# Second GEMM of blocks 2 to 8 by seven quarter-block products (Strassen's way) in a fused retention and feed-forward kernel

## The chip, the cores and the metric

The kernel runs on one core of a Trainium2 chip. The metric is the device time of one launch in microseconds. It is given as the median of several runs; one execution was taken with the hardware profiler.

The engines are named as the profile names them: PE is TensorE's matrix multiply, PEld its weight load, DVE is VectorE, ACT is ScalarE, POOL is GpSimd, and SP is the engine that here only issues transfers. Each engine works through its own instructions in the order in which the program gives them.

## The reference

A retention layer (attention without softmax, with a decay by distance) is followed by a feed-forward layer with a hard-swish between its two matrix products:

```python
# q, k, v: (8, 8, 576, 64) float32
scores = (1 / sqrt(64)) * q @ k.transpose(0, 1, 3, 2)
gamma = 1 - 2 ** (-5 - arange(8))                  # one per head
Dmat = where(rel >= 0, gamma ** rel, 0)            # rel = row - column
x = (scores * Dmat) @ v                            # -> (4608, 512) after a transpose of heads
h = x @ w_in                                       # (4608, 512) @ (512, 2048)
g = h * clip(h + 3, 0, 6) / 6
out = g @ w_out                                    # (4608, 2048) @ (2048, 512), float32
```

## The kernel before

All matrix work is in float16 with float32 accumulation in PSUM. The 4608 tokens are cut into nine blocks of 512, numbered 0 to 8. Blocks 0 to 7 are the first 512 tokens of each batch; block 8 is made of the last 64 tokens of all eight.

**Feed-forward.** `gemm1(kb)` makes the first product of block kb in 16 units. A unit (`g1`) is four matmuls of 512 columns into one PSUM bank `ph` (128 of the 2048 hidden columns, transposed), an ACT operation (Relu with a scale) into `u`, and a DVE operation (`scalar_tensor_tensor`) that writes 128 rows of `gt`, the hidden layer of the block, in float16. The second product (`g2`) takes `gt` as the stationary operand and `wout16` as the moving one. It makes four output tiles of 128 tokens x 512, each in 16 matmuls of 512 columns, cut into four parts: 16 units for a block. ACT copies each tile into `osb`, and SP stores it. In block 8 the last tile is made in two halves of 256 columns (`g2_halves`), so that the last copy and store are short.

**Retention.** It is cut into 36 pieces of 128 tokens: four for each batch, and four "rest" pieces of the last 64 tokens of two batches each. A piece is loaded by POOL's queue (`load`: k, q, v). `ahead(c)` prepares it: SP transposes k by DMA, DVE scales q and v in one operation of 1024 columns (`transpose_q`, line 294), and SP transposes the scaled q by DMA. The work proper is in steps. `step4(ended, begun)` finishes one group of pieces and begins the next, in this order on PE: `inter4(ended)` (what the running state gives, into banks o0 and o1), `scores4(begun)` (into `sc`), `update4(begun)` (the change of the state, into `tu` and a bank u1), `intra4(ended)` (what the masked scores give, added to o0 and o1). `outputs4(ended)` then copies o0 and o1 by ACT to the tokens of the next block in `xt16`. On DVE a step leaves the state's sums (`th`, `ta`, `ts`) and, between them, the mask of the scores (`at`, line 418); on ACT, beside the outputs, small copies `tm` of the state.

**Order.** The order is written out by hand. `put(units, steps)` runs a list of units and, after unit j, what `steps[j]` lists (j = -1: ahead of the first). The tables `steps_at` and `ahead_at` place the steps and the preparations in the second GEMM of each block, and `in_gemm1` places preparations and loads in the first. The retention of block kb + 1 runs inside the second GEMM of block kb. `load_from_here` has a group of loads begin only at a given matmul.

**PSUM.** There are eight banks: two for `sc`, one each for `o` and `tu`, and four that go round under the tag `ph`. These four serve the units of both GEMMs and, in every step, o1 and u1. A bank is written again when its last reader is done. `sc` exists once, so a step's scores wait for the mask of the step before.

Of the kernel before, what the change touches and what calls it, by code (L numbers as in the profile page):

```python
# [10 lines left out]
FP32 = mybir.dt.float32  # L11
# [6 lines left out]
def kernel(  # L18
# [59 lines left out]
    wout16 = big.tile([P, NFC, DM], FP16)  # L78
    xt16 = big.tile([P, NCC, NTOK], FP16)

# [90 lines left out]
    def warm(n, cols):  # L171

        w = psum.tile([P, MBLK], FP32, tag="ph", bufs=4, name=f"warm_{warmed[0]}")
        warmed[0] += 1
        for _ in range(n):
            nc.tensor.matmul(w[:, 0:cols], zeros[:, 0:P], zeros[:, 0:cols],
                             start=True, stop=True)
# [34 lines left out]

    def k_by_pe(c, tag="ph"):
        kn = loaded[c]["kn"]
        pk = psum.tile([P, NPAIR, P], FP16, tag=tag, bufs=4 if tag == "ph" else 1,
                       name=f"trk_{c}")
        for p in range(NPAIR):
            nc.tensor.transpose(pk[:, p, :], kn[:, 2 * p:2 * p + 2, :], ident16)  # L218
        nc.scalar.copy(qk_of(c)[:, 1], pk)  # L219

    def q_by_pe(c):
        q16, qk = loaded[c]["q16"], qk_of(c)
        pq = psum.tile([P, NPAIR, P], FP32, tag="ph", bufs=4, name=f"trq_{c}")
        for p in range(NPAIR):
            for h2 in range(2):
                r = slice(h2 * HALF, h2 * HALF + HALF)
                nc.tensor.matmul(pq[r, p, :], q16[:, 2 * p + h2, :], dq[:, 2 * p + h2, :],
                                 start=(p == 0), stop=(p == NPAIR - 1), skip_group_check=True)
        if c == EARLY - 1:
            for p in (0, 2):  # L230
                nc.scalar.copy(qk[:, 0, p:p + 2], pq[:, p:p + 2])
        else:
            nc.scalar.copy(qk[:, 0], pq)
# [17 lines left out]
    def out_last(c):  # L251
        before, qk = st[c]["before"], st[c]["qk"]
        at, vs = st[c]["at"], st[c]["vs"]
        g0 = column_of(c)
        halves = [psum.tile([P, NPAIR, P], FP32, tag="o", name=f"o_{c}"),
                  psum.tile([P, NPAIR, P], FP32, tag="ph", bufs=4, name=f"o2_{c}")]
        for i, o in enumerate(halves):
            for p in range(2):
                nc.tensor.matmul(o[:, p, :], tbd[before][:, 2 * i + p, :], qk[:, 0, 2 * i + p, :],
                                 start=(p == 0), stop=False, skip_group_check=True)  # L260
        for i, o in enumerate(halves):
            for p in range(2):
                for h2 in range(2):
                    r = slice(h2 * HALF, h2 * HALF + HALF)
                    nc.tensor.matmul(o[r, p, :], vs[:, 4 * i + 2 * p + h2, :],
                                     at[:, h2, 2 * i + p, :],
                                     start=False, stop=(p == 1), skip_group_check=True)
            nc.scalar.copy(xt16[:, 2 * i:2 * i + 2, g0:g0 + P], o[:, 0:2, :])

# [43 lines left out]
    def inter(c, tag="o"):  # L313
        kind, b, i, _ = pieces[c]
        o = psum.tile([P, NPAIR, P], FP32, tag=tag, bufs=4 if tag == "ph" else 1, name=f"o_{c}")
        st[c]["o"] = o
# [12 lines left out]
    def intra(c, copy_later=False, more=False):  # L329
        o, at, vs = st[c]["o"], st[c]["at"], st[c]["vs"]  # L330
        for p in range(NPAIR):
            for h2 in range(2):
# [3 lines left out]
                                 stop=(p == NPAIR - 1 and not more), skip_group_check=True)  # L336
        g0 = column_of(c)

        def copy():
            nc.scalar.copy(xt16[:, :, g0:g0 + P], o)  # L340

# [86 lines left out]
    def inter4(cs):  # L428

        o = [psum.tile([P, 2, NPAIR, HALF], FP32, tag="o", name=f"o0_{cs[0]}"),  # L430
             psum.tile([P, 2, NPAIR, HALF], FP32, tag="ph", bufs=4, name=f"o1_{cs[0]}")]
        written = set()
# [39 lines left out]
    def outputs4(cs):  # L472
        o, g0 = st[cs[0]]["o"], column_of(cs[0])
        if len(cs) == 2 and column_of(cs[1]) == g0 + P:
            for half in range(2):
                nc.scalar.copy(  # L476
                    xt16[:, :, g0:g0 + 2 * P].rearrange("e p (j x s) -> e p j x s", j=2, x=2)
                    [:, :, :, half, :], o[half].rearrange("e j p s -> e p j s"))
        else:
            for j, c in enumerate(cs):  # L480
                for half in range(2):
                    g0 = column_of(c) + half * HALF
                    nc.scalar.copy(xt16[:, :, g0:g0 + HALF], o[half][:, j])

    def update4(cs):

        cs = [c for c in cs if pieces[c][0] != "rest"]
        if not cs:
            return
        u = [psum.tile([P, 2, NPAIR, D], FP32, tag="tu", name=f"u0_{cs[0]}"),  # L490
             psum.tile([P, 2, NPAIR, D], FP32, tag="ph", bufs=4, name=f"u1_{cs[0]}")]
        for j, c in enumerate(cs):
# [46 lines left out]
    def g1_mm(kb, ph, fc, dmcs):  # L539
        t0 = kb * MBLK  # L540
        for dmc in dmcs:
            newest[0] = nc.tensor.matmul(  # L542
                ph, win16[:, dmc, P * fc:P * fc + P], xt16[:, dmc, t0:t0 + MBLK],
                start=(dmc == 0), stop=(dmc == NCC - 1))
# [9 lines left out]
    def g1_bank(kb, fc):  # L554
        return psum.tile([P, MBLK], FP32, tag="ph", bufs=4, name=f"ph_{kb}_{fc}")

    def g1(kb, fc, tag=None):
        ph = psum.tile([P, MBLK], FP32, tag=tag, name=f"ph_{kb}_{fc}") if tag else g1_bank(kb, fc)
        g1_mm(kb, ph, fc, range(NCC))
        g1_act(kb, ph, fc)  # L560

    def g1_columns(kb, fc, ph, cols):

        t0 = kb * MBLK
        for dmc in range(NCC):
            nc.tensor.matmul(ph[:, cols], win16[:, dmc, P * fc:P * fc + P],  # L566
                             xt16[:, dmc, t0 + cols.start:t0 + cols.stop],
                             start=(cols.start == 0 and dmc == 0),
# [26 lines left out]
    def g2(kb, mc, part):  # L595
        gt = gts[kb]
        if part == 0:
            pouts[kb, mc] = psum.tile([P, DM], FP32, tag="ph", bufs=4, name=f"pout_{kb}_{mc}")
        pout = pouts[kb, mc]
# [7 lines left out]

    def g2_halves(kb, mc):
        gt = gts[kb]
        W = DM // 2  # L610
        for half in range(2):
            pout = psum.tile([P, W], FP32, tag="ph", bufs=4, name=f"pout_{kb}_{mc}_{half}")
            for fc in range(NFC):
                nc.tensor.matmul(pout, gt[:, fc, P * mc:P * mc + P],  # L614
                                 wout16[:, fc, half * W:half * W + W],
                                 start=(fc == 0), stop=(fc == NFC - 1))
            osb = work.tile([P, W], FP32, tag="osh", bufs=2, name=f"osb_{kb}_{mc}_{half}")
            nc.scalar.copy(osb, pout)
            store(kb, mc, slice(half * W, half * W + W), osb)

# [63 lines left out]
    def first_step(c):  # L684
# [3 lines left out]
        if old:  # L688
            before = state_of.get(b)
            tag, bufs = ("ph", 4) if c == 6 else ("o", 1)  # L690
            o = psum.tile([P, NPAIR, P], FP32, tag=tag, bufs=bufs, name=f"o_{c - 1}")
            st[c - 1].update(o=o, first=True)
# [16 lines left out]
        if new:  # L709
            k_by_pe(c + 1, "ph" if old else "tu")  # L710
        if old:
# [16 lines left out]
    def scores_second(c):  # L728

        qk = st[c]["qk"]  # L730
        banks = [psum.tile([P, NPAIR, P], FP32, tag="ph", bufs=4, name=f"sc{i}_{c}")
                 for i in range(2)]
# [15 lines left out]
    def step(ended, begun):  # L748

        for c, tag in zip(ended, ("o", "ph")):  # L750
            inter(c, tag)
# [91 lines left out]
    i = 0  # L843
    for kb, at in ((2, (4, 8, 12)), (3, (4, 11)), (4, (3, 7, 12)), (5, (4, 11)), (6, (2, 8))):
        for j in at:
            steps_at.setdefault(kb, {})[j] = [(step4, groups[i], groups[i + 1])]
            i += 1
    steps_at[6][12] = [(inter4, groups[i]), (inter_done, groups[i])]
    steps_at[6][13] = [(end4, groups[i])]

    ahead_at = {1: {10: (12,), 11: (13,), 13: (14,), 14: (15,)}, 2: {1: (17,), 3: (18,)},
                3: {0: (21,), 1: (22,), 7: (23,), 8: (24,)}, 4: {0: (27,), 1: (28,)},
                5: {0: (31,), 1: (32,)}, 6: {0: (35,)}}
# [3 lines left out]
                5: {0: [(load_from_here, 29, 32)], 9: [(ahead, 29)], 12: [(ahead, 30)]},  # L857
                6: {0: [(load_from_here, 33, 35)], 9: [(ahead, 33)], 12: [(ahead, 34)]}}
    for kb in range(1, NMB - 1):
        steps = steps_at.get(kb, {})  # L860
        for j, cs in ahead_at.get(kb, {}).items():
            steps.setdefault(j, []).extend((ahead, c) for c in cs)
        put([unit2(kb, mc, part) for mc in range(MBLK // P) for part in range(4)], steps)
        gts.pop(kb)
        gemm1(kb + 1, in_gemm1.get(kb + 1, {}))
    for mc in range(MBLK // P - 1):
        for part in range(4):
            g2(NMB - 1, mc, part)
    g2_halves(NMB - 1, MBLK // P - 1)

# [29 lines left out]
```

## Time and profile before

| | us |
|---|---|
| median of 3 runs (306.27 to 307.74) | 306.35 |
| span of the profiled execution, first to last instruction | 303.8 |
| median less that span | 2.55 |

The profiled execution has no time of its own beside its span; what lies around the span is taken as the difference to the median.

| engine | busy us | share of the span | instructions |
|---|---|---|---|
| PE | 294.0 | 97% | 3035 |
| PEld | 146.4 | 48% | 3035 |
| DVE | 178.5 | 59% | 308 |
| ACT | 167.8 | 55% | 303 |
| POOL | 107.7 | 35% | 134 |

The mean granted clock of TensorE is 0.998. From block 2 on, each first GEMM takes 13.81 to 14.4 us; a second GEMM without retention steps (block 7) takes 13.81 us, and one with them 16.69 to 18.35 us.

A line of groups in the profile reads: source line, engine, operation, output<-inputs, shape, count | busy time, mean ns of one | idle time of the engine before them and what ended it. A line of a timeline reads: start, length, engine, line, operation. Durations of PE overlap (a matmul of 512 columns shows 379 ns, though one starts every 216), so its prices are taken from spacing.

### The profile page before, as it was taken

The page shows a single profiled execution, that of the slowest core. Times are in us where ns is not written, and L with a number is a line of the kernel's source. Part 1 is how long each engine was busy: PE and PEld are TensorE (multiplying, and loading weights), DVE is VectorE, ACT ScalarE, POOL GpSimd, SP SyncE. Part 2 cuts the span into 40 slices and gives each one's busy share as a digit, 9 for nine tenths or more (in the row PEclk, how much of TensorE's full clock was granted, in tenths as well). Part 3 has the DMA queues.
Part 4 walks back from the last instruction along what each step waited for, and adds up shares of the span by engine and source line. Part 5 has one row for each costly group of instructions (what it writes and reads, how often), then busy time and mean ns, then how long its engine had stood idle before and what let it go on. Part 6 is the DMA issues. An engine that isn't in the chain of part 4 may idle for free.

```text
span 303.8 us, 7342 instructions
## 1 busy us (share of the span) xinstructions
PE 294.0 (97%) x3035; PEld 146.4 (48%) x3035; DVE 178.5 (59%) x308; ACT 167.8 (55%) x303; POOL 107.7 (35%) x134
## 2 busy tenths in 40 slices
PE   6989999999999999999999999999999999999994
PEld 2644445544544555445544554445445444444443
DVE  4667526796838775966388767942895057108600
ACT  5557537874467455753585548633773367227511
POOL 8963557359840302930191009600840000000000
PEclk9999999999999999999999999999999999999999
DMA  9999999999999972999599619992992100010022
GB/s 69 144 193 206 190 156 209 163 120 151 187 173 146 155 126 83 116 120 174 142 128 178 115 37 127 140 151 74 107 150 74 71 37 0 35 73 32 1 69 71
DMA packets 153169, 35.61 MB, mean 117 GB/s; under 512 B 143792, under 2 KB 148656, under 8 KB 153136
## 3 DMA queue, kind: packets, MB, share of 16 engines
q0 software_dynamic: 117264, 18.36, 88.7%
q1 hardware_dynamic: 35472, 16.26, 29.6%
q8 instruction: 24, 0.39, 0.5%
q10 hardware_dynamic: 400, 0.52, 0.5%
q14 instruction: 9, 0.07, 0.1%
HBM read 36.70 MB, written 9.44 MB: 152 GB/s over the span
## 4 chain that ended last, share of the span: by engine, by line
PE 87%; DMA 5%; POOL 4%; issue 1%; DVE 1%; ACT 0%; DVEq 0%; POOLq 0%
PE pout L601 39%; PE ph L542 38%; DMA win<-in_moe_w_in_dram 3%; POOL qv L91 2%; DMA qk<-vs 2%; PE o L445 2%; PE o L466 1%; POOL kn L91 1%; PE ph L566 1%; PE sc L412 1%; PE pout L614 1%; PE u L498 1%; PE o L334 1%; PE sc L305 1%; POOL win L95 0%
## 5 line engine op out<-in xcount | busy, mean ns | idle before, releaser
L551 DVE SCALAR_TENSOR_TENSOR gt<-u,ph 128x512 f16<-128x512 f32 x144 | 97.3, 687 | 51.8 <-ACT u L550 50.5
L601 PE MATMUL pout<-wout,gt 128*128 128x512 f16 x560 | 125.9, 379 | 0.0
L542 PE MATMUL ph<-xt,win 128*128 128x512 f16 x560 | 122.7, 379 | 1.0 <-DMA win<-in_moe_w_in_dram 1.0
L550 ACT ACTIVATE u<-ph,cb 128x512 f32<-128x512 f32 x144 | 98.3, 687 | 27.1 <-PE ph L542 26.4
L542 PEld LDWEIGHTS <-win 128*128 128x128 f16 x560 | 54.6, 98 | 67.1 <-DMA win<-in_moe_w_in_dram 1.9
L601 PEld LDWEIGHTS <-gt 128*128 128x128 f16 x560 | 53.1, 98 | 61.5
L91 POOL DMA_DIRECT2D kn<-in_k_dram x40 | 35.3, 887 | 102.8 <-PE ph L542 75.7
L605 ACT COPY osb<-pout 128x512 f32<-128x512 f32 x35 | 20.5, 585 | 60.7 <-PE pout L601 60.7
L91 POOL DMA_DIRECT2D qv<-in_q_dram x40 | 35.2, 885 | 5.3 <-DMA wout<-in_moe_w_out_dram 3.3
L91 POOL DMA_DIRECT2D qv<-in_v_dram x40 | 35.5, 894 | 3.6 <-DMA win<-in_moe_w_in_dram 1.7
L294 DVE TENSOR_TENSOR vs<-qv,gqv 128x1024 f16<-128x1024 f16 x28 | 18.7, 686 | 4.7 <-issue 3.5
L309 DVE TENSOR_TENSOR at<-sc,mask_wide 128x1024 f16<-128x1024 f32 x9 | 11.0, 1222 | 14.1 <-PE sc L305 14.0
L529 DVE TENSOR_TENSOR ta<-u,th 128x256 f32<-128x256 f32 x20 | 8.4, 420 | 12.5 <-ACT th L517 11.7
L418 DVE TENSOR_TENSOR at<-sc,mask 128x1024 f16<-128x1024 f32 x11 | 13.4, 1216 | 2.4 <-PE sc L412 2.4
L514 DVE TENSOR_TENSOR th<-u,ts 128x256 f32<-128x256 f32 x15 | 6.4, 425 | 11.6 <-PE u L498 11.2
L476 ACT CAST xt<-o 128x512 f16<-128x512 f32 x16 | 8.6, 589 | 6.4 <-PE o L466 6.4
L519 ACT CAST tm<-th 128x256 f16<-128x256 f32 x20 | 8.2, 412 | 2.8 <-DVE th L514 2.4
L530 DVE TENSOR_TENSOR ts<-ta,gc 128x256 f16<-128x256 f32 x20 | 8.5, 425 | 0.7
L340 ACT CAST xt<-o 128x512 f16<-128x512 f32 x11 | 6.3, 588 | 3.5 <-PE o L707 1.7
L219 ACT COPY qk<-trk 128x512 f16<-128x512 f16 x8 | 4.7, 586 | 4.7 <-PE trk L218 4.6
L412 PE MATMUL sc<-qk 64*64 64x64 f16 x384 | 6.5, 195 | 0.7 <-DMA qk<-vs 0.7
L457 ACT COPY seen<-o 128x1 f32<-128x1 f32 x13 | 2.1, 159 | 9.0 <-PE o L445 8.9
(90 smaller groups left out, 159.2 us busy)
## 6 DMA issues: line engine op xcount, KB each, us to landing
out_dram<-osb SPq DMA_DIRECT2D x32, 256.0 KB, 2.2
kn<-in_k_dram POOLq DMA_DIRECT2D x32, 128.0 KB, 5.9
qv<-in_q_dram POOLq DMA_DIRECT2D x32, 128.0 KB, 5.9
qv<-in_v_dram POOLq DMA_DIRECT2D x32, 128.0 KB, 6.6
wout<-in_moe_w_out_dram POOLq DMA_DIRECT2D x4, 512.0 KB, 15.2
win<-in_moe_w_in_dram POOLq DMA_DIRECT2D x3, 512.0 KB, 11.7
win<-in_moe_w_in_dram POOLq DMA_DIRECT2D x2, 256.0 KB, 7.4
kn<-in_k_dram POOLq DMA_DIRECT2D x8, 64.0 KB, 4.1
```

The costliest lines, as they stand in the source:

```text
L91: loaded[c]["dma"].append(nc.gpsimd.dma_start(dst[p0:p0 + n], src[b, :, s0:s0 + n, :].rearrange("h s d -> s h d")))
L294: scaled = nc.vector.tensor_tensor(out=vs, in0=loaded[c]["qv"], in1=gqv, op=ALU.mult)
L309: later.append(lambda: nc.vector.tensor_tensor(out=at.rearrange("t a b s -> t (a b) s"), in0=sc.rearrange("t a b s -> t (a b) s"), in1=mas ...
L412: nc.tensor.matmul(sc[rows(half), h2, j, p, :], qk[rows(h2), 1, p, rows(half)], qk[rows(h2), 0, p, rows(half)], start=True, stop=True)
L418: nc.vector.tensor_tensor(out=at.rearrange("t a j p s -> t (a j p) s"), in0=sc.rearrange("t a j p s -> t (a j p) s"), in1=mask64[:, None, ...
L476: nc.scalar.copy(xt16[:, :, g0:g0 + 2 * P].rearrange("e p (j x s) -> e p j x s", j=2, x=2) [:, :, :, half, :], o[half].rearrange("e j p s ...
L530: nc.vector.tensor_tensor(out=ts, in0=ta, in1=scale, op=ALU.mult)
L542: newest[0] = nc.tensor.matmul(ph, win16[:, dmc, P * fc:P * fc + P], xt16[:, dmc, t0:t0 + MBLK], start=(dmc == 0), stop=(dmc == NCC - 1))
L550: nc.scalar.activation(u, ph, ACTF.Relu, bias=cb[:, 0:1], scale=1.0 / 6.0)
L551: nc.vector.scalar_tensor_tensor(out=gts[kb][:, fc, :], in0=u, scalar=1.0, in1=ph, op0=ALU.min, op1=ALU.mult)
L601: nc.tensor.matmul(pout, gt[:, fc, P * mc:P * mc + P], wout16[:, fc, :], start=(fc == 0), stop=(fc == NFC - 1))
L605: nc.scalar.copy(osb, pout)
```

## The change

Blocks 2 to 8 make their second product as follows. The block's hidden layer (512 tokens x 2048) is cut into quarters a(i, j) of 256 tokens x 1024, the weights into quarters w(i, j) of 1024 x 256. In place of eight products of quarters, seven are made, of sums of quarters: s1 to s4 from the hidden layer, made on DVE for each block (`token_sums`), and t1 to t4 from the weights, made once on DVE during block 1's second GEMM (`weight_sums`). Each product is two units of eight matmuls of 256 columns, so a second GEMM has 14 units and 112 matmuls.

Four PSUM banks serve the products, by name: x (three products, one added to the other), z (two), y and v (one each). `bank` hands out the four `ph` banks in turn and passes over those that are held; x and z are held to the end of the block. ACT copies x out after each of its three products (`keep`: m1, u2, u3, float32), and DVE adds such a copy to y, z, v and again z (`total`), which gives the four quarters of the output. Each is stored in one transfer with rows of 1 KB (`store_quarter`). In block 8, z is in the two banks of `sc`, and the last quarter is added and stored in two halves.

`token_sums` s1 and s2 are made in two halves each, behind units 12, 13 and 15 of the block's first GEMM; s3 and s4 are made during the second. The retention steps and some preparations stand behind other units than before. The one large `xt16` gives way to tiles by block (`xt_of`), two in turn and one for block 8; this makes room in SBUF.

```diff
+    def bank(shape, dtype, name):
+        i = next(x for x in ring if x not in held)
+        ring.remove(i)
+        ring.append(i)
+        return psum.tile(shape, dtype, tag=f"ph{i}", name=name)
+    def hold_bank():
+        held.append(ring[-1])
+    def free_banks():
+        for i in held[1:]:
+            ring.remove(i)
+            ring.append(i)
+        held.clear()
...
+        a, b, op = {"t1": (w(0, 1), w(0, 0), ALU.subtract),
+                    "t2": (w(1, 1), t("t1"), ALU.subtract),
+                    "t3": (w(1, 1), w(0, 1), ALU.subtract),
+                    "t4": (w(1, 0), t("t2"), ALU.subtract)}[which]
+        nc.vector.tensor_tensor(out=t(which), in0=a, in1=b, op=op)
...
+    def token_sums(kb, which, c0=0, c1=KH):
...
+                sums[kb, name] = work.tile([P, KH, TH], FP16, tag="sum_" + {"s4": "s1"}.get(name, name), bufs=1,
+                                           name=f"sum_{name}_{kb}")
...
+        x, y, op = {"s1": (lambda: a(1, 0), lambda: a(1, 1), ALU.add),
+                    "s2": (lambda: s("s1")[:, c0:c1], lambda: a(0, 0), ALU.subtract),
+                    "s3": (lambda: a(0, 0), lambda: a(1, 0), ALU.subtract),
+                    "s4": (lambda: a(0, 1), lambda: s("s2")[:, c0:c1], ALU.subtract)}[which]
+        nc.vector.tensor_tensor(out=s(which)[:, c0:c1], in0=x(), in1=y(), op=op)
...
+        def product(name, u, left, right, first):
+            dst = get(name)
+            for c in range(KH):
+                nc.tensor.matmul(dst[:, u, :], left()[:, c, P * u:P * u + P], right[:, c, :],
+                                 start=(first and c == 0 and (u == 0 or last and name == "z")),
+                                 stop=(c == KH - 1), skip_group_check=True)
...
+        def keep(name, src):
+            kept[name] = work.tile([P, 2, NH], FP32, tag="keep_" + {"u3": "m1"}.get(name, name), bufs=1,
+                                   name=f"keep_{name}_{kb}")
+            nc.scalar.copy(kept[name], get(src))
+        def total(i, j, name, src):
+            osb = work.tile([P, 2, NH], FP32, tag="osb", bufs=4, name=f"osb_{kb}_{i}_{j}")
+            nc.vector.tensor_tensor(out=osb, in0=get(src), in1=kept[name], op=ALU.add)
+            store_quarter(kb, i, j, osb)
...
+        plan = [
+            ("x", lambda: a(0, 0), w(0, 0), True, [lambda: keep("m1", "x")]),
+            ("y", lambda: a(0, 1), w(1, 0), True,
+             [lambda: total(0, 0, "m1", "y"), lambda: token_sums(kb, "s3")]),
+            ("x", lambda: s("s2"), wts["t2"], False,
+             [lambda: keep("u2", "x")]),
+            ("z", lambda: s("s1"), wts["t1"], True, [lambda: token_sums(kb, "s4")]),
+            ("x", lambda: s("s3"), wts["t3"], False,
+             [lambda: keep("u3", "x"), lambda: total(1, 1, "u3", "z")]),
+            ("v", lambda: a(1, 1), wts["t4"], True, [lambda: total(1, 0, "u3", "v")]),
+            ("z", lambda: s("s4"), w(1, 1), False, [] if last else
+             [lambda: total(0, 1, "u2", "z"), free_banks]),
+        ]
...
-    for kb, at in ((2, (4, 8, 12)), (3, (4, 11)), (4, (3, 7, 12)), (5, (4, 11)), (6, (2, 8))):
+    for kb, at in ((2, (1, 5, 9)), (3, (3, 9)), (4, (1, 5, 9)), (5, (3, 9)), (6, (1, 7))):
...
-    steps_at[6][12] = [(inter4, groups[i]), (inter_done, groups[i])]
-    steps_at[6][13] = [(end4, groups[i])]
+    steps_at[6][10] = [(inter4, groups[i]), (inter_done, groups[i])]
+    steps_at[6][11] = [(end4, groups[i])]
-    ahead_at = {1: {10: (12,), 11: (13,), 13: (14,), 14: (15,)}, 2: {1: (17,), 3: (18,)},
-                3: {0: (21,), 1: (22,), 7: (23,), 8: (24,)}, 4: {0: (27,), 1: (28,)},
+    ahead_at = {1: {10: (12,), 11: (13,), 13: (14,), 14: (15,)}, 2: {0: (17,), 2: (18,)},
+                3: {0: (21,), 1: (22,), 5: (23,), 6: (24,)}, 4: {1: (27,), 2: (28,)},
                 5: {0: (31,), 1: (32,)}, 6: {0: (35,)}}
...
+    for j, which in ((2, "t1"), (4, "t2"), (9, "t3"), (10, "t4")):
+        steps_at[1].setdefault(j, []).append((weight_sums, which))
+    SEVEN = (2, 3, 4, 5, 6, 7, 8)
...
+            if kb + 1 in SEVEN:
+                for j, which in ((12, "s1"), (13, "s2")):
+                    within.setdefault(j, []).append((token_sums, kb + 1, which, 0, KH // 2))
+                for which in ("s1", "s2"):
+                    within.setdefault(15, []).append((token_sums, kb + 1, which, KH // 2, KH))
```

## The prediction

> **What bounds the kernel now.** I read the page's busy shares, then the windows view over the alternating stretches of the two GEMMs (cut where the matmuls' line changes), then the groups by form, the chain and timelines. Times are in us unless marked ns; T is the start of a block's second GEMM.
>
> ```profile
> PE 294.0 (97%) x3035; PEld 146.4 (48%) x3035; DVE 178.5 (59%) x308; ACT 167.8 (55%) x303; POOL 107.7 (35%) x134
> ```
> ```profile
> 118.56:132.37 13.81, 13.81 (x66) 6.27 (x64) 12.20 (x19) 11.06 (x17) 11.97 (x15) 1.00 1.45 120
> 132.37:149.06 16.69, 16.69 (x297) 8.68 (x296) 9.45 (x16) 6.32 (x15) 0.00 (x0) 1.00 1.53 141
> 149.06:162.87 13.81, 13.81 (x65) 6.27 (x64) 10.35 (x16) 10.86 (x16) 10.49 (x12) 1.00 1.95 145
> 162.87:181.22 18.35, 18.35 (x434) 10.08 (x432) 12.09 (x23) 8.60 (x23) 0.00 (x0) 1.00 0.77 109
> ...
> 195.03:212.61 17.58, 16.93 (x305) 8.81 (x304) 6.89 (x13) 6.45 (x17) 0.00 (x0) 1.00 0.88 118
> ...
> 257.88:271.69 13.81, 13.81 (x65) 6.27 (x64) 1.37 (x2) 2.46 (x5) 0.00 (x0) 1.00 0.15 58
> ```
>
> Columns: stretch, length, busy PE, PEld, DVE, ACT, POOL, granted clock, DMA. Rows: both GEMMs of block 3, both of 4, the second of 5 and of 7. PE idles only in block 5 (0.65): TensorE is the bound, and time taken off it is gained unless a wait takes its place. DVE is the engine to watch: block 3 uses 12.20 + 9.45 = 21.65 of 30.50.
>
> ```profile
> L601 PE MATMUL pout<-wout,gt 128*128 128x512 f16 x560 | 125.9, 379 | 0.0
> ...
> L551 DVE SCALAR_TENSOR_TENSOR gt<-u,ph 128x512 f16<-128x512 f32 x144 | 97.3, 687 | 51.8 <-ACT u L550 50.5
> L294 DVE TENSOR_TENSOR vs<-qv,gqv 128x1024 f16<-128x1024 f16 x28 | 18.7, 686 | 4.7 <-issue 3.5 <-DMA qv<-in_v_dram 1.2
> ...
> L137 DVE TENSOR_TENSOR dq<-ident,gq 128x1024 f16<-128x1024 f16 x1 | 1.2, 1226 | 0.3 <-ACT gq L125 0.3
> ```
> ```profile
> 296.03 3.51 PE pout L614 x32
> ```
>
> Prices: 64 matmuls of 512 columns fill 13.81, 215.8 ns each. In the chain the 32 of 256 columns take 3.51, 109.7 ns each. On DVE a 1024-element f16 operation costs 686 ns.
>
> ```profile
> 138.13 4.71 PE L601 MATMUL pout<-wout,gt 128*128 128x512 f16 x21
> ...
> 138.43 1.07 ACT L476 CAST xt<-o 128x512 f16<-128x512 f32 x2 [0.88 <-PE o L466]
> ...
> 141.32 0.42 DVE L530 TENSOR_TENSOR ts<-ta,gc 128x256 f16<-128x256 f32 x1
> 141.66 1.28 DVE L294 TENSOR_TENSOR vs<-qv,gqv 128x1024 f16<-128x1024 f16 x2
> ...
> 200.91 0.32 PE L412 MATMUL sc<-qk 64*64 64x64 f16 x16 [0.65 <-DMA qk<-vs]
> ```
>
> These timeline rows (start, length) give the rest: a step's outputs are out of PSUM 0.30 + 1.07 after PE has gone on to the next product; a queued DVE operation starts 0.08 before the last one ends (141.66 against 141.74), so 686 ns counts 603 in a full queue; and block 5's step already waits for a transposed q.
>
> **The change, part by part.**
>
> *Products.* A block loses 64 x 215.8 ns = 13.81 and gets 112 x 109.7 = 12.29: -1.52. Block 8 had 48 x 215.8 and 32 x 109.7 = 13.87: -1.58. Seven blocks: **-10.7**, all on PE. This rests on L614's pitch, which hides a weight load of 98 ns with 12 to spare. [...]
>
> *VectorE.* New per block: s1 and s2 in halves (4 x 0.603), s3 and s4 of 2048 elements (512 f16 elements take 418 ns in L205's row, 1024 take 686, so 2048 take 1.22, 1.14 in a queue), four totals from PSUM (L551's size, 4 x 0.603): 7.1. ACT keeps three copies for four: -0.6, hidden. Block 3: 21.65 + 7.1 = 28.8 of 30.50 - 1.52 = 29.0; block 4: 22.4 + 7.1 = 29.5 of 30.6; block 7: 18.9 of 26. So DVE is full in blocks 2 to 4, and its queue, in order, decides who waits. The weight sums (4 x 1.14) fall in block 1's second GEMM, where DVE is busy 10.4 of 16.6: nothing; without that cover, 4.6.
>
> *Banks.* x and z hold two of the four banks. In blocks 2 to 5 the step behind unit 9 takes both others, and v, next on PE, gets the one of the step's o1: it waits for ACT's copies out of it. Price 0.30 + 1.07 = 1.4 (block 3); four narrow copies (L483: 384 ns, 300 for each further one) make it 1.6 in 4 and 5; two make 1.0 in 2: **+5.6**. Before, the bank after a step's was drained long ago.
>
> *Block 2.* DVE's order behind the first GEMM: the last hard-swish product (ACT starts at T + 0.20, takes 0.69, DVE follows 0.17 later, and 0.42 late through the first halves of s1 and s2), the second halves (to T + 3.3), then the mask of the step that opens the block (ends T + 4.5). The next step moves from behind unit 4 (T + 4.8) to behind unit 1 (T + 2.2), and its scores need the one sc tile: PE is there at T + 2.6, **+1.9**, with products y and on queued behind. DVE now runs late: that step's th, ta, ts, th, mask, ta, ts (3.7 by their rows), piece 18's scaling, and only then total 00 at T + 10.2; z gets y's bank and waits **0.75**.
>
> *Block 4.* Likewise: second halves to T + 3.9 (two scalings late in the first GEMM), step 3.7, scalings of 27 and 28 1.2, total 00 done at T + 9.6; PE wants z at T + 8.15: **+1.45**.
>
> *Transposes.* Steps come sooner after the first GEMM, transposes don't. Block 5: q of piece 30 lands at T + 5.85 (200.9), the step behind unit 3 asks at T + 4.3: 1.6, less the 0.65 of before. Block 3: q of 20 landed at T + 4.4, asked for at 3.9: 0.5. **+1.45**. On SP's queue total 00's store, which now waits on DVE, stands ahead of the transposes of 23 and 24; these have the next first GEMM for cover, without it some 2. POOL's loads keep their places.
>
> *Small ones.* Block 3's x waits for its ACT copy behind a step's state copies, 0.15; block 5's y for the last hard-swish product, 0.4; block 6's third pass on x for s3, 0.5; in blocks 7 and 8, z's last pass for ACT's copy and DVE's total (0.9 + 0.8 + hand-over) against v's 1.75, 0.1 each: **+1.25**. The tail is a copy and stores of the same size: nothing. Stores have rows of 1 KB for 2: DMA moves 58 GB/s in block 7, so nothing, at most 0.5 at the end.
>
> *Sum.* -10.7 + 5.6 + (1.9 + 0.75) + 1.45 + 1.45 + 1.25 = **+1.7** on the profile's span of 303.8: 305.5. The runs' median (306.35) is 2.55 above that span, start and end that the change doesn't touch: **308.0**. The waits, which the trace of before can't show, are bounded by nothing (-10.7) and about double (+14.1); I take the walk between, as its rows are of the same operations.
>
> **Rivals.**
> 1. *VectorE keeps up* (faster): only v's waits remain, as nothing stands between step and v: -10.7 + 5.6, **301.2**. For it: in blocks 6 to 8 DVE has a quarter of the time free. Against: 28.8 of 29.0 in block 3. Chance 0.30.
> 2. *Transposes become the bound* (slower): the scalings queue behind sums, so q of pieces 22 and 28 is issued up to 4 later and lands 2.6 (201.49 to 204.06) to 6 after issue. Blocks 3 and 4 need them behind unit 9, near T + 11.6 and T + 13.5, about when they land; from there each us late is a us. 1.5 each: **311.0**. Against: loads have ended by then, so 2.6 is the likelier. Chance 0.13.
> 3. *Sums at one element a cycle* (slower): L137, with one f32 operand, takes 1226 ns for 1024. At that rate sums cost 4.3 more a block; blocks 2 to 4 get DVE's own length (99.6 against 94.9 before), 5 to 8 wait some 2 each for s2 and save 1.5, and 5's v waits 1.6: **314.7**. It decides once a half sum exceeds 0.9. Against: the sums are f16 throughout, as L294. Chance 0.07.
> 4. *The clock drops* (slower): early warm-up matmuls start 427 ns apart (2.018, 2.445), half the later rate. If a stall in each of blocks 2 to 5 brought that back for 3.5, two products' time, each would lose 1.75: **315.0**. The longest gap in the trace is 0.77 and leaves clock 1.00; my longest wait is 1.9. [...] Chance 0.03.
> 5. *No PE time is saved* (slower): weight loads surface and cost 14 ns a matmul, 112 x 14 = 1.57 a block, so the waits alone remain: **318.7**. Against: L614. Chance 0.02.
>
> **How the numbers follow.** The walk has 0.45; with its 12.4 of waits off by 30% either way it spans 304 to 312. This kernel's measurement tells some 0.5% (1.5) from no change. Slower by more: half of the walk (0.23), rivals 3 to 5 (0.12) and most of 2 (0.10): 0.45. Faster: rival 1 and the low end of the walk, 0.34. Within: 0.21. The range 300 to 313 leaves out rivals 3 to 5 (0.12) and the far end of 1 (0.06).
>
> **What would show it.** Products: the second GEMMs of blocks 7 and 8 near 12.4. Banks: four PE waits of 1.0 to 1.6 on ACT's xt copies, just ahead of v. DVE: sums at 686 ns and 1.22; PE waiting for the mask in block 2, for total 00 in 2 and 4. I am wrong if blocks 3 to 5 shrink by 1.5 each (rival 1), or if a single wait exceeds 2.5.

## The result and the profile after

The changed kernel takes **309.90 us** (median of 4 runs, 308.47 to 310.76), the kernel before 306.31 on the same chip (4 runs). The ratio is 1.0122, with a 95% interval of 1.0087 to 1.0156: slower by 1.2%. The profiled execution has a span of 308.9 and is the longest of the four (the others: 306.6, 308.0, 308.2), so its 5.14 over the span of before is more than the 3.6 between the medians.

From the page of after: the engines, and the granted clock by fortieths of the span.

```profile
PE 285.4 (92%) x3355; PEld 179.3 (58%) x3355; DVE 233.6 (76%) x383; ACT 164.1 (53%) x297; POOL 107.7 (35%) x134
...
PEclk9599999999999999999999999997999999999999
```

PE was busy for 97% of its span, now for 92%: the work fell by 8.6, the span rose by 5.1. In the clock's row one slice near 210 has fallen to 7. The windows view (stretch, length, busy PE, PEld, DVE, ACT, POOL, granted clock, DMA) over the second GEMMs of blocks 2, 3, 4, 5, 7 and 8:

```profile
102.43:121.84 19.41, 16.59 (x434) 14.50 (x425) 17.77 (x32) 8.16 (x23) 2.63 (x3) 1.00 0.59 86
...
135.65:152.73 17.08, 15.30 (x346) 13.43 (x345) 15.35 (x25) 6.31 (x15) 0.00 (x0) 1.00 1.45 131
...
166.54:186.74 20.20, 16.92 (x482) 14.99 (x480) 19.34 (x34) 8.73 (x25) 0.00 (x0) 1.00 0.59 87
...
200.55:221.34 20.79, 17.25 (x354) 14.46 (x353) 14.40 (x24) 6.54 (x17) 0.00 (x0) 0.92 0.81 86
...
265.45:277.68 12.23, 12.23 (x113) 10.96 (x112) 7.84 (x11) 2.47 (x5) 0.00 (x0) 1.00 0.13 45
291.49:308.91 17.42, 12.56 (x113) 10.86 (x111) 8.68 (x13) 2.47 (x5) 0.00 (x0) 0.97 0.23 61
```

Block 7, where no retention step stands, takes 12.23 instead of 13.81: the seven products are 1.58 shorter, and 12.23 / 112 is 109.2 ns a matmul. Blocks 2 to 5 have 1.8 to 3.5 in which PE stands still. Block 5 has, besides, a clock of 0.92. The waits of PE (line, what it waited for: us in all, times, longest) name these idle times:

```profile
PE v L717 <- ACT xt L512: 3.4, 3, 1.4
PE sc L442 <- DMA qk<-vs: 3.2, 3, 2.2
PE z L717 <- DVE osb L730: 1.8, 2, 1.3
PE sc L442 <- DVE at L448: 1.6, 1, 1.6
PE ph L593 <- ACT osb L632: 1.2, 1, 1.2
PE v L717 <- ACT xt L506: 1.2, 1, 1.2
...
PE trq L259 <- ACT osb L632: 0.7, 1, 0.7
```

They are, in this order: v for the narrow copies out of a step's bank (0.7, 1.4 and 1.3 in blocks 2, 4 and 5); a step's scores for a transposed q (2.2 in block 5, 0.6 in block 4, 0.4 in block 6); z for the quarter total 00 (1.3 in block 4, 0.5 in block 2); block 2's scores for the mask; block 1's first `ph` for the copy of an output tile of block 0; v for the wide copies in block 3; and, inside block 0's second GEMM, another bank that ACT is still copying out of. All but the fifth and the last are of the kinds that the prediction names. The timeline of PE in block 5 (start, length, operation) shows the longest one and what follows it:

```profile
207.35 0.32 PE L442 MATMUL sc<-qk 64*64 64x64 f16 x16 [2.22 <-DMA qk<-vs]
...
208.01 2.95 PE L717 MATMUL x<-wsum_t,sum_s 128*128 128x256 f16 x16
210.76 2.59 PE L717 MATMUL z<-wsum_t,sum_s 128*128 128x256 f16 x16
213.19 1.91 PE L717 MATMUL x<-wsum_t,sum_s 128*128 128x256 f16 x16
...
217.85 1.36 PE L717 MATMUL v<-wsum_t,gt 128*128 128x256 f16 x11 [1.33 <-ACT xt L512]
```

Behind the wait of 2.2 a product takes 2.95 and 2.59 where one takes 1.91 later: the matmuls start 213 ns apart until 212.1, and 109 from there. The granted clock is 0.50 from 208.73 to 212.14, and that costs 1.7 (1.04 + 0.68).

By stages, in us from one change of the matmuls' line to the next (the first GEMMs and the second one of block 1 that are not listed are the same in both kernels):

| stage | before | after | forecast of the difference | measured |
|---|---|---|---|---|
| start and first GEMM of block 0 | 33.73 | 33.27 | 0 | -0.5 |
| second GEMM, block 0 | 20.10 | 22.25 | 0 | **+2.15** |
| block 2 | 17.82 | 19.41 | +2.1 | +1.6 |
| block 3 | 16.69 | 17.07 | +0.5 | +0.4 |
| block 4 | 18.35 | 20.20 | +1.5 | +1.9 |
| block 5 | 17.58 | 20.78 | +1.4 | **+3.2** |
| block 6 | 17.64 | 16.49 | -1.0 | -1.2 |
| block 7 | 13.81 | 12.23 | -1.4 | -1.6 |
| block 8 | 18.27 | 17.42 | -1.5 | -0.85 |

### The profile page after: what moved, and what is told of

Same layout as the page of the kernel before. It is cut to its first block, busy times and chain, and to the rows that moved or that the text cites. A ratio compares the mean times of both kernels' runs of the same rounds, so it can differ in the third digit from the quotient of the medians.

```text
span 308.9 us, 8057 instructions
## 1 busy us (share of the span) xinstructions
PE 285.4 (92%) x3355; PEld 179.3 (58%) x3355; DVE 233.6 (76%) x383; ACT 164.1 (53%) x297; POOL 107.7 (35%) x134
## 4 chain that ended last, share of the span: by engine, by line
PE 66%; DMA 14%; DVE 8%; POOL 5%; ACT 3%; issue 3%; DVEq 0%; POOLq 0%
PE ph L570 31%; PE x L717 9%; PE z L717 7%; DMA wout<-in_moe_w_out_dram 5%; PE pout L628 5%; PE v L717 4%; DMA qk<-vs 4%; DMA win<-in_moe_w_in_dram 3%; POOL qv L124 3%; PE y L717 3%; DVE sum_s L673 2%; DMA qv<-in_q_dram 2%; DVE gt L579 2%; POOL kn L124 1%; PE ph L593 1%
## 5 line engine op out<-in xcount | busy, mean ns | idle before, releaser
L717 PEld LDWEIGHTS <-sum_s 128*128 128x128 f16 x448 | 44.4, 100 | 9.2 <-issue 3.2
L717 PEld LDWEIGHTS <-gt 128*128 128x128 f16 x336 | 32.3, 98 | 10.1 <-issue 4.2
L628 PE MATMUL pout<-wout,gt 128*128 128x512 f16 x128 | 29.1, 379 | 0.0
L717 PE MATMUL x<-wsum_t,sum_s 128*128 128x256 f16 x224 | 27.8, 279 | 0.6 <-ACT keep_u L726 0.6
L628 PEld LDWEIGHTS <-gt 128*128 128x128 f16 x128 | 12.0, 98 | 13.4
L673 DVE TENSOR_TENSOR sum_s<-gt 128x1024 f16<-128x1024 f16 (+1 forms) x21 | 18.1, 864 | 0.2
L717 PE MATMUL v<-wsum_t,gt 128*128 128x256 f16 x112 | 13.5, 272 | 4.6 <-ACT xt L512 3.4
L730 DVE TENSOR_TENSOR osb<-z,keep_u 128x512 f32<-128x512 f32 x13 | 9.0, 689 | 9.0 <-ACT keep_u L726 5.1
L717 PE MATMUL z<-wsum_t,sum_s 128*128 128x256 f16 x112 | 14.0, 281 | 1.8 <-DVE osb L730 1.8
L717 PE MATMUL z<-wout,sum_s 128*128 128x256 f16 x112 | 13.5, 273 | 0.5 <-DVE osh L735 0.5
L717 PE MATMUL y<-wout,gt 128*128 128x256 f16 x112 | 13.6, 273 | 0.0
```

Source lines behind the costliest of these rows:

```text
L628: nc.tensor.matmul(pout, gt[:, fc, P * mc:P * mc + P], wout16[:, fc, :], start=(fc == 0), stop=(fc == NFC - 1))
L673: nc.vector.tensor_tensor(out=s(which)[:, c0:c1], in0=x(), in1=y(), op=op)
L717: nc.tensor.matmul(dst[:, u, :], left()[:, c, P * u:P * u + P], right[:, c, :], start=(first and c == 0 and (u == 0 or last and name == "z")),
L730: nc.vector.tensor_tensor(out=osb, in0=get(src), in1=kept[name], op=ALU.add)
```

## The experiments

The theory at the outset: the products save 1.58 in each block, and the waits in blocks 2 to 5, block 0's 2.15 and the half clock in block 5 take more than that back. The rivals: the new banks and tiles cost by themselves, wherever there are products; or VectorE is simply too full.

**The plumbing alone.** All of the new bank ring and tiles, the order of before, no block by seven products (`g2_halves` is put back for block 8).

```diff
-    SEVEN = (2, 3, 4, 5, 6, 7, 8)
+    SEVEN = ()
-    for kb, at in ((2, (1, 5, 9)), (3, (3, 9)), (4, (1, 5, 9)), (5, (3, 9)), (6, (1, 7))):
+    for kb, at in ((2, (4, 8, 12)), (3, (4, 11)), (4, (3, 7, 12)), (5, (4, 11)), (6, (2, 8))):
```

> The changed kernel's banks handed out in turn by hand and its token tiles by block, but no block in seven products, no weight sums, and all steps where they stood before. Theory (the hand-made turn of the banks gives block 1's first matmul the bank of block 0's last output tile, which is still being summed and copied): the second GEMM of block 0 grows by about 2.1 us and nothing else does, 308.4 us against 306.3. Rival (the new banks and tiles cost nothing, and the late start of block 2 in the changed kernel comes from the weight sums or from the loads): 306.3 us, the second GEMM of block 0 at 20.1 us.

Measured: 307.45, ratio 1.0068 (1.0037 to 1.01). Block 0's second GEMM is 22.25 here too, the blocks from 2 on are within 0.5 of before. So 2.15 of the loss has nothing to do with the products. The ring gives out the banks of blocks 0 and 1 in another order than the tag of before did. Twice that puts a tile into the bank whose output tile ACT is still copying: 0.7 is lost inside block 0's second GEMM (`trq`, at 43.41), and the other 1.4 at the change from block 0 to 1 (`ph`; timeline of PE in after):

```profile
55.52 1.46 PE L593 MATMUL ph<-xt,win 128*128 128x384 f16 x8 [1.25 <-ACT osb L632]
```

**The old banks in blocks 0 and 1.** The change whole, but the tiles up to the first steps of block 1 get, by name, the banks that they had before.

```diff
-        i = next(x for x in ring if x not in held)
+        i = OLD.get(name, next(x for x in ring if x not in held))
```

> One edit in the changed kernel: up to the end of block 1, each tile gets the bank that it had in the kernel before; from there the banks go in turn. Theory (the turn of the banks costs 2.1 us in block 0): the second GEMM of block 0 is back at 20.1 us and the kernel at 307.8 us. Rival (the loss of 1.7 us ahead of block 2 comes from the loads at the start, which differ from run to run): no change, 309.9 us.

Measured: 308.03, ratio 1.0064 (1.0025 to 1.0103). Block 0's second GEMM is back at 20.28. The profiled execution has two stretches of half clock, in blocks 2 and 5 (granted clock 0.50 in 104.67:108.08 and 207.07:210.48), which hide some of this in its span (307.2).

**Only the blocks without crowded steps.** Seven products in 6 to 8, and in 2 to 5 the order of before; then the same with the old banks.

```diff
-    SEVEN = (2, 3, 4, 5, 6, 7, 8)
+    SEVEN = (6, 7, 8)
```

> Seven products in blocks 6, 7 and 8 alone; blocks 2 to 5 in eight, with their steps where they stood before; weight sums kept. Theory (the products save 1.5 us a block, the waits behind the steps of blocks 2 to 5 take it back): blocks 6, 7, 8 give -1.15, -1.6 and -0.85 us as in the changed kernel, the banks of block 0 cost 2.1 us, so 304.8 us, some 5 us under the changed kernel. Rival (the saving is real in every block and the loss lies elsewhere): with four blocks fewer in seven products the kernel is slower than the changed one, 313 us or more.

> Seven products in blocks 6, 7 and 8 alone and the old banks up to block 1, together. Theory (the two effects add: the 303.3 us of the late blocks alone, less the 2.0 us that the turn of the banks costs in block 0): 301.3 us. Rival (a later start only moves waits into the loads): 303 us.

Measured: 303.33, ratio 0.9925 (0.9897 to 0.9953); with the old banks 301.57, ratio 0.9866 (0.9815 to 0.9917). Both theories hold, the first with 1.5 to spare (304.8 was expected). In blocks 6 to 8 the products pay (16.24, 12.23 and 17.40 us), and blocks 2 to 5 are what the change loses.

**The bank of x given back.** x is dead once its third copy is out, but stays held to the end of its block, so v gets the bank of the step's o1. Here x's bank goes back at that point, and v takes it.

```diff
+    def free_x():
+        i = held.pop(0)
+        ring.remove(i)
+        ring.append(i)
...
-             [lambda: keep("u3", "x"), lambda: total(1, 1, "u3", "z")]),
+             [lambda: keep("u3", "x"), free_x, lambda: total(1, 1, "u3", "z")]),
```

> One edit in the changed kernel: once u3 is copied out of x, x is no longer held and goes to the end of the turn, so that v takes x's bank and not the bank of the step's o1. Theory (v waits for the copies out of o1 and nothing else stands behind them): the waits of v in blocks 2 to 5 (0.7, 1.2, 1.2, 1.1 us of idle PE) go, and the kernel gains 4 to 5 us: 305 to 306 us. Rival (VectorE is full in these blocks, so PE waits for a total or a sum a little later instead): a gain under 1.5 us, 308.5 us or more, with new waits of z's last pass on the total of z and u3.

Measured: 307.51, ratio 1.0045 (1.0011 to 1.0079), where 305 to 306 was expected. All four waits of v are gone; but of their 4.6 only about half comes back. Blocks 2, 3 and 5 get 0.79, 1.26 and 1.35 shorter, which is v's wait in each, block 4 only 0.32, and block 6 and the first GEMM ahead of it grow by 1.32. In block 4 (PE's waits there) the scores of the last step now wait for the transposes of piece 28:

```profile
PE sc L447 <- DMA qk<-vs: 1.3, 1, 1.3
```

That step stands ahead of v, so v's wait in this block can't have covered it. In this execution the q of pieces 27 and 28 lands 11.9 and 15.5 into block 4, against 10.8 and 14.4 in after. Two versions below have the same edit, and there block 4's wait for a transposed q is 0.3 and the block takes 18.54 and 18.56, so block 4's small gain here goes with the late transfers of this execution, and not with the bank; why they are late is not shown. Block 6's growth comes back in both.

**The sums left out.** s1 to s4 are made for block 2 alone; blocks 3 to 8 use those of block 2, so their output differs and VectorE has some 4.7 less to do in each.

```diff
     def token_sums(kb, which, c0=0, c1=KH):
+        if kb > 2:
+            sums[kb, which] = sums[2, {"s1": "s4"}.get(which, which)]
+            return
```

> The changed kernel, but s1 to s4 are made for block 2 alone, and the products of blocks 3 to 8 read these same sums: 4.7 us less of VectorE's work in each of blocks 3 to 8, nothing moved on PE, on the banks or in the transposes. Theory (late totals and sums are one part of the waits, banks and transposes the other): block 4 loses its wait of z for the total of y (1.3 us) and block 3 its 0.6, while v's waits for the copies out of o1 and block 5's wait for a transposed q stay; blocks 3, 4, 5 near 16.5, 18.5, 19.5 us, the kernel near 306.5 us. Rival (VectorE's load is all of the loss): blocks 3 to 5 come down to 15.2, 16.8, 15.4 us, the kernel to 300 us.

Measured: 308.06, ratio 1.0103 (1.002 to 1.0186). Blocks 3, 4 and 5 take 16.52, 19.72 and 21.35, against 17.07, 20.20 and 20.78 with the sums. PE's waits on DVE for total 00 fall from 1.8 to 0.8 in all (1.3 to 0.35 in block 4; block 2's stays, as its sums are made), and block 3's wait for x's copy goes. The waits for banks stay, and those for transposes grow: from 0.6 to 1.1 in block 4, which was expected near 18.5, and from 2.2 to 3.0 in block 5:

```profile
PE sc L442 <- DMA qk<-vs: 4.6, 3, 3.0
PE v L720 <- ACT xt L512: 3.4, 3, 1.4
```

So without the sums' load on VectorE blocks 3 and 4 gain about half a us each, and block 5 nothing. This refutes the rival. It also limits the prediction's own "DVE is full [...] and its queue, in order, decides who waits": that holds for total 00, and not for the waits that make up most of the loss.

**Two placements.** Both bank repairs (the old banks in blocks 0 and 1, and x's bank given back), block 2's second halves of s1 and s2 moved behind its opening step, and block 5's first step moved from unit 3 to unit 5; then the same with the last step of blocks 2 to 5 behind unit 11.

```diff
-    for kb, at in ((2, (1, 5, 9)), (3, (3, 9)), (4, (1, 5, 9)), (5, (3, 9)), (6, (1, 7))):
+    for kb, at in ((2, (1, 5, 9)), (3, (3, 9)), (4, (1, 5, 9)), (5, (5, 9)), (6, (1, 7))):
...
-                    within.setdefault(15, []).append((token_sums, kb + 1, which, KH // 2, KH))
+                    where = steps_at[2][-1] if kb + 1 == 2 else within.setdefault(15, [])
+                    where.append((token_sums, kb + 1, which, KH // 2, KH))
```

> The changed kernel with the old banks up to block 1, x's bank freed for v, and two moves: in block 2 the second halves of s1 and s2 come behind the step that opens its second GEMM (its mask first), and in block 5 the step behind unit 3 stands behind unit 5. Theory (each wait of PE is one item in a queue that stands ahead of what PE wants, and goes when that item is moved): block 2's second GEMM falls from 18.6 us (x's bank freed) to about 17.0, block 5's from 19.4 to about 16.5, and with no gap of 2 us left in block 5 TensorE's clock stays whole; 301 to 302 us. Rival (VectorE is full in blocks 2 to 5 and PE waits for it somewhere in any order): blocks 2 and 5 stay within 0.5 us of 18.6 and 19.4, the kernel at 305 us.

> As the kernel with two moves, and besides the last step of blocks 2 to 5 stands behind unit 11 (behind v), not behind unit 9. Theory (the step behind unit 9 asks for transposed q and k before they land, 1.3 us in block 4, and two units of v, 1.75 us, give them the time): block 4 falls from 19.9 to about 18.5 us, the others stay or gain up to 0.5 us; 299 to 300.5 us. Rival (what is late is VectorE's work for the step, which now runs into the next block's first GEMM): the first GEMMs of blocks 3 to 6 grow beyond 13.81 us by 0.5 us or more each, and the kernel is not faster than the one with two moves.

Measured: 302.22, ratio 0.9875 (0.9816 to 0.9933), and 303.06, ratio 0.9952 (0.9912 to 0.9992). The first total is near the 301 to 302 that was expected, though its blocks are not; the second, expected at 299 to 300.5, is no faster than the first, as its rival had it. In the first, block 2 takes 18.49 where 17.0 was expected: the mask's wait shrinks from 1.6 to 0.4, but z's wait for total 00 grows from 0.45 to 1.1, as the halves of the sums now stand ahead of that. Block 5 takes 18.37 where 16.5 was expected: its step stands two units (16 x 109 ns, 1.75) later, and still waits 1.9 for a transposed q, which here lands 8.40 into the block, against 6.76 in after (PE's waits in blocks 2 and 5):

```profile
PE z L723 <- DVE osb L736: 1.1, 1, 1.1
PE sc L448 <- DVE at L454: 0.4, 2, 0.3
...
PE sc L448 <- DMA qk<-vs: 1.9, 1, 1.9
```

With the last steps later, block 5 falls to 16.55, but the first GEMMs behind blocks 2 and 5 grow to 14.48 and 15.03, since their units wait for DVE's late state sums (1.2 in all). So the state sums that were put off on VectorE are met again in the next stage.

**Why block 5's transposes are late.** In after, q of piece 30 is issued at 200.34 and lands at 207.31; in the kernel before, 194.81 and 200.87. Each time that is within 0.3 of when the last of the loads of pieces 29 to 32 lands (207.03; 200.69). These are held to block 5's first GEMM. In the next two runs (all seven blocks, both bank repairs) they are issued behind the last step of block 4: first without a hold, then held to the matmul behind unit 10.

```diff
-                5: {0: [(load_from_here, 29, 32)], 9: [(ahead, 29)], 12: [(ahead, 30)]},
+                5: {9: [(ahead, 29)], 12: [(ahead, 30)]},
...
+    steps_at[4][9].append((load_until, 32))        # first run
+    steps_at[4][10] = [(load_from_here, 29, 32)]   # second run; product() sets newest[0]
```

> All seven blocks in seven products, old banks, x's bank freed, and the loads of pieces 29 to 32 begin behind the last step of block 4, some 5 us sooner, instead of at the first matmul of block 5. Theory (the transposes of piece 30 land only with the last of these loads, and block 5's step waits for them): block 5's second GEMM falls from 19.4 us to 16.5 us or less, and TensorE's clock stays whole there; block 4 may wait up to 1 us more, as its transposes then share the queues with the loads. Rival (the transposes are late because VectorE scales q late): block 5 stays above 18.5 us.

> All seven blocks with x's bank given back and the old banks in blocks 0 and 1; the loads of pieces 29 to 32 are held to the matmul behind unit 10 of block 4's second GEMM, so they begin behind that block's last step and no longer at block 5's first GEMM. In the run without the hold they began some 18 us too early, beside block 4's transposes, and block 5's second GEMM still fell to 15.35. Theory (block 5 is long because its transposes land behind these loads): block 4 is back at 19.9 (x's bank given back alone), block 5 stays at 15.4, the granted clock is whole up to the tail; span 299.2, time 301.2. Rival (the loads cost wherever they stand): block 4's last step or its stores are late by 1 or more, or block 6 takes up what block 5 saves (17.9 becomes 19); span 301 or more, time 303.

Without the hold: 309.07, ratio 1.0131 (1.0083 to 1.0179), not what was expected. POOL did not wait for PE's place in the program: with nothing to hold them, the loads followed those of 25 to 28 at once, from 159.2 on, while the step that they stand behind began at 180.4. So they ran beside block 4's transposes. Windows over the second GEMMs of blocks 4 and 5:

```profile
161.16:189.83 28.67, 21.94 (x482) 17.56 (x480) 19.79 (x34) 8.62 (x25) 10.23 (x13) 0.82 1.79 129
203.64:218.99 15.35, 15.35 (x353) 13.37 (x352) 12.85 (x21) 6.44 (x17) 0.00 (x0) 1.00 0.58 84
```

q of piece 27 then landed 14.0 us into block 4 (10.8 in after and with the hold, 11.9 with x's bank given back alone). PE waited 2.5 and 2.2 in two steps, for what the trace doesn't name, and 1.9 for a late sum, and the granted clock was 0.82 over block 4, as much as three stretches of 3.41 at 0.50 take off: the block takes 28.67. That the early loads are behind this is shown by the second run, which differs by the hold alone. But block 5 has no wait left, and takes 15.35 for 19.43, which refutes the rival. With the hold both come right: **300.79**, ratio 0.9867 (0.9844 to 0.989), block 4 at 18.56 and block 5 at 15.36. PE's waits from 160 to 220:

```profile
PE z L723 <- DVE osb L736: 1.3, 1, 1.3
PE sc L448 <- DMA qk<-vs: 0.3, 1, 0.3
```

The theory's span was 299.2, the run's is 299.0; that they are so close is in part chance, as block 4 was expected at 19.9. From after to this version the stages give back 2.16 (block 0), 0.79, 1.24, 1.64 and 5.42 (blocks 2 to 5), take 1.51 (block 6 and the first GEMM ahead of it) and differ by 0.19 at the start: 9.93 of the 9.94 between the two spans.

**Seven products where they pay.** Blocks 3, 6, 7 and 8, both bank repairs, elsewhere the order of before.

> Seven products in blocks 3, 6, 7 and 8; old banks up to block 1; x's bank freed for v; blocks 2, 4 and 5 in eight products with their steps where they stood before. Theory (a block gains its 1.5 us where no wait takes it back; block 3 came to 15.8 us against 16.7 with x's bank freed): 0.9 us less than seven products in blocks 6 to 8 with the old banks, 300.7 us, ratio to the kernel before 0.982 to 0.985. Rival (with step and v closer together in block 3 the transposes of block 4 come late): no faster than 301.6 us.

Measured: **300.55**, ratio 0.986 (0.9818 to 0.9902). By their ratios this, the run before it (0.9867) and seven products in blocks 6 to 8 alone with the old banks (0.9866) cannot be told apart, so the 0.9 that block 3 was to add is not shown: in the profiled executions block 3 takes 15.84 for 16.90, but blocks 5 and 6 together 1.2 more. All three are faster than either kernel.

**Waits put in by hand.** Does the half clock come with PE's waits? In the kernel before, three are put where PE has none: in block 7, and in block 8's first GEMM. ACT copies a PSUM tile (six copies for the long wait), and PE needs the copy.

```diff
+    steps_at[7] = {3: [(gap, lambda: pouts[7, 0], 0)], 11: [(gap, lambda: pouts[7, 2], 5)]}
+    in_gemm1[8] = {7: [(gap, lambda: gts[8][:, 7, :], 0)]}
```

> The kernel before with three waits put on PE where it has none: in block 7's second GEMM a matmul behind unit 3 that waits for one more ACT copy (about 1.5 us of idle PE) and one behind unit 11 that waits for six (about 4 us), and in block 8's first GEMM one behind unit 7 that waits for a copy of gt (about 2.5 us); the values computed are the reference's. [...] Rival (half clock in the changed kernel came from something else, load or temperature): granted clock 1.00 throughout, at most 8 us more.

Measured in one execution (span 315.7): waits of 1.2, 4.1 and 2.2. Behind the first, 32 matmuls of 512 columns take 7.07, some 216 ns apart: the clock stays whole. With the other two the granted clock is 0.50, with the second one for two stretches of 3.41 (from 271.84 to 278.67, while the wait ends at 273.55) and with the third for one (from 288.91). That refutes the rival. In the windows (second number: busy PE; the number third from the right: granted clock), a stretch with little PE work comes first and the half clock in the next one:

```profile
268.43:271.84 3.41, 1.00 (x5) 0.37 (x4) 0.00 (x0) 2.27 (x5) 0.00 (x0) 1.00 0.20 77
271.84:275.26 3.42, 1.71 (x5) 0.59 (x5) 0.00 (x0) 1.63 (x3) 0.00 (x0) 0.50 0.00 0
275.26:278.67 3.41, 3.41 (x9) 1.18 (x8) 0.00 (x0) 0.00 (x0) 0.00 (x0) 0.50 0.02 5
285.50:288.91 3.41, 1.26 (x8) 0.52 (x6) 2.06 (x3) 2.10 (x4) 0.00 (x0) 1.00 0.01 2
288.91:292.32 3.41, 3.41 (x10) 1.22 (x8) 0.69 (x1) 0.69 (x1) 0.00 (x0) 0.50 0.00 0
```

## Why the prediction was nearly right, step by step

- *Products*, -10.7: right. Block 7 shows -1.58 against -1.52, so -11.1 over seven blocks. A matmul takes 109.2 ns at 256 columns, with a weight load for each (112 in block 7), and 215.8 at 512.
- *Banks*, +5.6: right in kind and place, a little large. The four waits of v come to 4.6 (3.4 + 1.2), and they vanish when x's bank is given back.
- *Block 2*, 1.9 for the mask: 1.6. 0.75 for total 00: 0.45; z begins at T + 10.4, and the walk had total 00 done at T + 10.2.
- *Block 4*, 1.45 for total 00: 1.3; z begins at T + 9.63, against T + 9.6. The walk through VectorE's queue was right.
- *Transposes*, +1.45: too small, about 2.5 (3.2 in all, less the 0.7 of before). Block 3's 0.5 doesn't show; block 5 has 1.6 more than before where 0.95 was forecast, and blocks 4 and 6 wait 0.6 and 0.4. The step took the landing in block 5, T + 5.85, from the trace of before; this q lands within 0.3 of the loads in front of it, and in the changed kernel that is T + 6.76 (7.0 to 7.3 with the old banks, with x's bank given back and with the sums left out). Why these loads land later is not shown. Of the second rival's transposes, those of piece 22 cost nothing and those of 28 cost 0.6, not 1.5 each.
- *Small ones*, +1.25: x in block 3 waits 0.6 for its copy, not 0.15; z in block 8 0.5, not 0.1; the 0.4 of y in block 5 and the 0.5 for s3 in block 6 don't show. Block 8 saves 0.85 where 1.48 was forecast; 0.2 of that is left unexplained.
- *What it says nothing of*: block 0. The prediction works out what the new `bank` does in blocks 2 to 8 only, though every tile of the tag passes through it: 2.15. This is the largest term missed.
- *The clock*, the fourth rival: it took part in block 5, for 1.7. The prediction gave it 0.03, by a longest gap of 0.77 and a longest wait of 1.9. That gap ends at 5.13 in the trace of before, where matmuls of 128 columns start 107 ns apart, against 56 at 12.6, so it doesn't show that a gap leaves the clock whole. The longest wait became 2.22, and the granted clock was 0.50 in the stretch behind it; the made wait of 2.15 was followed by 0.50 too.
- *VectorE*: its second-GEMM shares (17.77 of 19.41 in block 2, 19.34 of 20.20 in block 4) are as full as forecast, but with the sums left out in blocks 3 to 8 the time hardly changes (ratio 1.0103, against 1.0122). Of PE's waits in after, those for the mask, total 00 and x's copy, 4.0 together, hang on VectorE's and ACT's queues; those for banks and transposed tiles are 9.8, with block 0's.

The forecast's +1.7 against +5.1 in the profiled execution, or +3.6 between the medians, is thus the sum of block 0 (+2.15) and block 5's clock (+1.7), both left out, and smaller errors of both signs. The mechanism forecast for blocks 2 to 8 is the one that the runs show; that 309.90 still fell within 300 to 313, with two terms of 3.9 together left out, is in part luck.

## What to carry to other kernels

A saving on the bound engine (here 11 us of PE) is worth what its new waits leave of it, and each of those has a place: here a bank held past its last reader, an order of banks changed for stages that the edit does not mean to touch, and loads that stand ahead of the transposes that a step needs. When a wait is taken away, look for the next one: with x's bank given back, blocks 2, 3 and 5 got their wait of v back, and block 6 and the first GEMM ahead of it took 1.3 of that, in part because a step there waited longer for a transposed tile (0.9 for 0.4). Here moving work within VectorE's queue mostly moved the wait (block 2's mask against total 00, the last steps against the next first GEMM); giving back the bank and moving the loads ended theirs.

## What the runs showed of the hardware

- *The granted clock changed at points that lie multiples of 3.413 us apart.* In after it changes at 14.17, 208.73, 212.14 and 307.71: 57, 1 and 28 times 3.413 apart. Behind stretches of that length with 1.37 and 0.26 us of busy PE (in after), 1.08 (with x's bank given back), 1.42 (with the sums left out), 1.78 and 1.39 (with the old banks), and 1.00, 1.71 and 1.26 (with the made waits) the granted clock was 0.50. Behind 1.94 (in after) and 2.21 (in the run with two placements) it was 1.00, and behind 1.92 (that run, block 5) a product took 1.91, as at the whole clock. Where a limit lies, and whether the busy time alone sets it, these runs do not show. The longest wait alone doesn't tell: block 2's scores wait 1.6 for the mask in after and with the old banks alike. In after 1.94 of that stretch (102.91:106.33) is busy, and the clock stays whole; with the old banks 1.78 is, block 2's next longest wait is 0.7, and half clock follows (the two rows below).

```profile
101.25:104.66 3.41, 1.78 (x124) 1.46 (x122) 3.34 (x6) 0.66 (x2) 1.42 (x2) 1.00 1.53 98
104.67:108.08 3.41, 3.41 (x17) 2.45 (x17) 3.17 (x7) 1.90 (x6) 0.00 (x0) 0.50 0.56 76
```

- *The transposes by DMA took longer with loads under way.* Issue to landing of the q of piece 30 is 7.0 behind the loads (200.34 to 207.31, after), and 4.0 with none under way (203.34 to 207.35, in the run without the hold); for piece 29 it is 5.8 (197.61 to 203.41) and 2.4 (200.70 to 203.14). Against the start of block 5's second GEMM the q of piece 30 lands at 5.8 to 6.2 in four versions that make blocks 4 and 5 in eight products, and at 6.8 to 8.4 in six that make them in seven with the loads where they were, so a landing taken from another version is known no better than that.
- *POOL's transfers did not keep PE's place in the program where no dependency tied them.* Without one, the loads put behind the last step of block 4 began 21 us ahead of it (159.2 against 180.4).
